# Linear attention and a gated MLP on one core: a new order for TensorE, K weights ahead of Q weights, and two tiles that are centred before the first projection

## The chip, the cores and the metric

The kernel runs on one core of a Trainium2 chip. The metric is device microseconds for one execution; the time before is the median of three runs. The engines of a core work side by side, each through its own list of instructions: TensorE (PE: matmuls and transposes), VectorE (DVE), ScalarE (ACT), GpSimd (POOL) and SyncE (SP), which here only issues DMA transfers. They wait for each other through semaphores. An order that differs between two kernels can therefore change the time although no instruction is added or taken away.

## The reference, cut to what matters

```python
def _layernorm(x):                     # over the last axis, eps = 1e-5
    return (x - mean(x)) / sqrt(var(x) + eps)

# x: 2048 x 448 bf16, 16 heads of 28; wqkv: 448 x 1344; wo: 448 x 448
q, k, v = split(_layernorm(x) @ wqkv)             # per head
phi = lambda t: where(t > 0, t + 1, exp(t)) + 1e-6
pq, pk = phi(q), phi(k)
kv  = pk^T v                                      # per head, 28 x 28, over all rows
z   = sum of pk over all rows
o   = (pq @ kv) / (pq . z + 1e-6)
h   = x + o @ wo
# w_gate, w_up: 448 x 1792; w_down: 1792 x 448
g, u = _layernorm(h) @ w_gate, _layernorm(h) @ w_up
out = h + (gelu(g) * u) @ w_down
```

`kv` needs all rows of K before any attention output can be formed. So the kernel first does K for all 16 tiles of 128 rows, and then attention output, gate/up and down projections tile by tile.

## The kernel before: the parts that matter

Every instruction is a task with a name, an engine and the buffers that it reads and writes. A table gives the order of the tasks on each engine; a task waits by semaphores for those on other engines that it depends on.

```python
ORDERS = ("26 34 32 43 41 63 ...", ...)     # PE, ACT, DVE, POOL, SP: task numbers

b_wqk = bufs("wqk", 2)                      # rows 0-383, and the tail of 64 rows
dma_x("sp", 0, 1)                           # x tile 0
tx1 = dma_x("act", 1, 2)                    # x tile 1
dma_w3("sp", wqk_sb, 0, 2 * D, b_wqk, "dwqk")     # Q and K weights, rows 0-383
dma_w1("sp", wqk_sb, 0, 2 * D, b_wqk, "dwqk_t")   # their tail
dma_x("sp", 2, 4); dma_x("sp", 4, 8); dma_x("sp", 8, 12); dma_x("sp", 12, 16)
# ... V weights, output weights

WARM = 40                                   # matmuls on a tile of ones
SEQ = "Q0 K0 K1 Q1 K2 Q2 K3 K4 K5 Q3 K6 K7 K8 ..."

def ln_tile(t):
    ln_stats(t, ...)                        # bn_stats, bn_aggr on DVE
    ln_rstd_act(t, ...)                     # ACT: Ln(var + eps), Exp(-0.5 * .)
    if t < N_PE_TR:                         # tiles 0 to 3
        # DVE: xnn = (x - mean) * rstd
        # PE: transpose by identity into two PSUM banks
        # ACT evacuates chunks 0 and 1, DVE chunks 2 and 3, into xnT
    else:
        # POOL: xnn = (x + negmean) * rstd
        # SP: transposing DMA xnn -> xnT

def k_tile(t):
    # PE: psK = xnT . wk (4 matmuls of 448 columns)
    # ACT: e1 = Exp(psK)
    # DVE: e1 = max(min(e1, 1 + EPS), 0)
    # DVE: pk = max(psK, EPS) + e1
    # PE: pt += xnn^T . pk (4 matmuls), accumulated over all tiles
def q_tile(t):
    # PE: psQ = xnT . wq;  ACT: eq = Exp(psQ), pq = Relu(psQ)
# ... (cut) kv and w2, the product of kv and wo

def a2_pair(p):                             # two tiles of attention output
    # DVE/POOL: pq, denominator, pqn; SP: transposing DMA oT (p > 0)
    # PE: out (8 matmuls, K = 112); DVE: h = x + out, statistics
    # POOL: normalisation; DVE: wrap (a copy); SP: transposing DMA hT

def gu_chunk(t0, nt):                       # groups of gate/up: 28 pairs of N=256 or 14 of N=512
    # PE: pairs on 64 rows each: psG on rows 0-63, psU on rows 64-127
    # ACT: gl = Gelu(psG); DVE: hh = psU * gl  (two halves)
def b2_tile(t):
    # PE: down, 14 matmuls of 448 columns; DVE: out = down + h; SP: store
```

Tiles 0 and 1, 2 and 3 form the gate/up groups 0 to 13 (28 pairs each), tiles 4 to 7 the groups 14 to 27, tiles 8 to 11 the groups 28 to 41, tiles 12 to 15 the groups 42 to 55 (14 pairs each). Gate and up have two PSUM banks each, used in turn. In the profile, L342 is the warm-up, L378 the transpose by TensorE, L404 a Q or K projection, L423 the accumulation of `pt`, L523 the attention output, L603 and L605 gate and up, L575 the down projection; L348 is the statistics, L370 the normalisation on VectorE, L390 the transposing DMA of a tile.

Of the kernel before, what the change touches and what calls it, by code (L numbers as in the profile page):

```python
# [5 lines left out]
BF16 = mybir.dt.bfloat16  # L6
F32 = mybir.dt.float32
ALU = mybir.AluOpType
# [7 lines left out]
    "26 34 32 43 41 63 66 71 76 50 52 61 59 79 84 70 87 116 75 99 83 111 91 126 103 138 150 115 130 162 174 142 187"  # L16
    " 200 154 213 219 229 166 245 178 191 235 204 217 179 233 249 192 205 218 234 250 254 251 291 257 295 297 293"
    " 299 263 315 266 317 319 260 320 269 278 275 272 333 337 356 434 439 387 444 449 454 459 418 464 506 472 516"
    " 511 526 521 469 490 531 536 578 583 588 562 544 593 598 603 608 613 675 541 618 623 628 633 638 643 706 651"
    " 648 657 654 722 727 732 737 742 747 752 757 762 767 772 777 782 787 804 809 814 795 792 801 798 819 824 829"  # L20
    " 834 839 844 849 854 859 864 869 874 877 880 883 886",
    "3 25 29 30 38 39 33 42 65 47 48 56 67 57 64 51 94 72 95 60 78 106 80 107 85 86 121 122 88 77 133 134 145 146"
    " 118 182 100 157 158 169 117 112 183 170 127 139 195 196 208 224 225 209 240 241 151 163 175 188 201 214 220"
    " 221 230 246 236 237 285 308 289 288 312 252 347 253 256 259 298 351 255 294 316 264 318 268 258 265 262 267"
    " 261 327 328 271 329 330 379 383 279 273 280 334 270 276 274 277 339 437 435 440 442 410 414 447 445 450 452"
    " 457 455 460 462 465 467 482 507 509 486 558 517 519 514 512 527 554 529 524 522 534 532 537 539 671 581 579"
    " 586 667 584 589 591 698 594 596 599 601 702 604 606 609 611 614 616 621 619 624 626 629 631 636 634 639 641"
    " 644 646 723 725 730 728 735 733 738 740 743 745 748 750 753 755 758 760 763 765 770 768 773 775 778 780 783"
    " 785 790 788 805 807 812 810 817 815 820 822 827 825 830 832 835 837 842 840 845 847 852 850 855 857 862 860"
    " 867 865 870 872",  # L30
    "27 28 36 37 31 40 35 44 45 54 46 55 104 49 92 58 93 68 53 69 105 73 62 74 119 131 120 143 81 144 180 132 181"
    " 89 82 167 155 90 156 168 101 193 102 222 194 113 223 114 340 128 206 129 238 207 303 239 140 141 301 152 302"
    " 153 164 165 176 177 189 202 342 190 343 215 216 341 203 231 372 232 247 248 304 374 373 375 287 286 305 307"
    " 309 290 311 310 313 346 292 350 296 378 348 352 314 300 349 353 321 405 322 324 323 325 475 326 331 382 332"
    " 335 384 336 380 385 381 338 403 406 404 360 357 361 358 409 362 359 413 436 438 411 415 441 443 412 416 367"
    " 476 448 446 388 547 549 451 453 391 370 389 458 390 477 392 548 478 456 461 393 463 419 693 550 485 481 422"
    " 466 468 508 510 420 553 423 487 424 401 691 398 557 421 662 483 518 520 488 515 559 513 663 484 429 560 555"
    " 523 525 692 432 670 660 528 530 661 473 491 494 556 694 535 533 538 540 666 495 582 580 492 470 587 672 493"
    " 496 697 585 590 566 563 668 669 673 564 592 567 565 595 597 701 568 699 600 703 602 605 607 704 545 612 504"
    " 700 615 573 617 679 676 610 680 677 542 678 681 622 620 625 627 576 501 630 632 637 635 640 707 710 642 645"  # L40
    " 708 711 709 712 686 647 652 649 717 720 658 724 726 655 731 729 736 734 739 741 744 746 689 749 751 754 756"
    " 759 761 764 766 771 769 774 776 779 781 784 786 791 789 806 808 813 811 818 816 796 793 799 802 821 823 828"
    " 826 831 833 836 838 843 841 846 848 853 851 856 858 863 861 868 866 871 873 875 878 881 884 887",
    "17 15 13 0 18 14 20 16 1 21 24 19 23 96 97 108 109 123 124 135 147 136 22 148 159 171 184 160 172 197 185 226"
    " 198 210 242 211 227 243 306 344 345 376 377 408 407 364 363 365 366 479 369 480 395 394 396 400 551 552 397"
    " 426 425 427 428 665 431 664 696 695 498 497 499 500 503 570 569 571 572 575 683 682 684 685 688 714 713 715"
    " 716 719",
    "2 4 5 6 7 8 9 10 11 12 98 110 125 137 149 161 173 186 199 212 228 244 281 282 283 284 354 386 355 417 368 371"
    " 402 399 489 430 433 474 561 471 674 505 574 705 543 546 502 577 687 653 718 721 650 656 659 690 797 794 800"
    " 803 879 876 882 885 888",  # L50
# [120 lines left out]
def bass_sequential_preLN__linear_attn_block__glu_gated_geglu__prompt_kernel(  # L171
# [11 lines left out]
    N_PE_TR = 4  # L183
    B1_CHUNKS = [2, 2, 4, 4, 4]
    WARM = 40
    T1_DVE = (0,)
    SEQ = "Q0 K0 K1 Q1 K2 Q2 K3 K4 K5 Q3 K6 K7 K8 K9 K10 K11 K12 K13 Q4 K14 Q5 K15 Q6 Q7 Q8 Q9 Q10 Q11 Q12 Q13 Q14 Q15"

    G = _Graph()
    es = ExitStack()  # L190
    with es:
        block = es.enter_context(nc.Block())

        def sb(name, shape, dt):
            return es.enter_context(nc.sbuf_tensor(name, shape, dt))

        x_sb = sb("x_sb", [128, T, D], BF16)
        xnn = sb("xnn", [128, XN_R, 512], BF16)
        xnT = sb("xnT", [128, T, 4, 128], BF16)
# [45 lines left out]
        def bufs(name, n):  # L245
            return [_Buf("%s%d" % (name, i)) for i in range(n)]

        b_x = bufs("x", T)
        b_xn = bufs("xn", XN_R)
        b_xnT = [bufs("xnT%d_" % t, 2) for t in range(T)]  # L250
        b_ones2 = _Buf("ones2")
        b_wqk, b_wv = bufs("wqk", 2), bufs("wv", 2)
# [48 lines left out]
        for dst, b, nm_ in ((wqk_sb, b_wqk, "wqkpad"), (wv_sb, b_wv, "wvpad")):  # L301
            op("pool", lambda e, dst=dst: e.memset(dst[:, 3, :], 0.0), [], [b[1]], nm_)  # L302
        dma_x("sp", 0, 1)
        tx1 = dma_x("act", 1, 2)
        dma_w3("sp", wqk_sb, 0, 2 * D, b_wqk, "dwqk")
        dma_w1("sp", wqk_sb, 0, 2 * D, b_wqk, "dwqk_t")
        dma_x("sp", 2, 4)
        dma_x("sp", 4, 8)
# [18 lines left out]
           [b_mtmp], [b_mask], "mask_b")  # L327
        op("pool", lambda e: e.memset(pt_sb[:, 3, :], 0.0), [], [b_pt[3]], "ptpad")
# [10 lines left out]
        def warm_fn(e):  # L339
            ins = None  # L340
            for _ in range(WARM):
                ins = e.matmul(ps[:, 3, 0:128], ones_bf[:], ones_bf[:], start=True, stop=True)  # L342
            return ins
        G.add("pe", warm_fn, r=[b_ones], w=[b_ps[3]], name="warm")
# [20 lines left out]
        def ln_tile(t):  # L365
# [3 lines left out]
            if t < N_PE_TR:  # L369
                op("dve", lambda e: e.tensor_scalar(xnn[:, i, 0:D], x_sb[:, t, :], mv1[:, t, 0:1], rs1[:, t:t + 1], ALU.subtract, ALU.mult),  # L370
                   [b_x[t], b_mv1[t], b_rs1[t]], [b_xn[i]], "normD_%d" % t)
                for h, (eng, k0, k1) in enumerate((("act", 0, 2), ("dve", 2, 4))):
                    bk = BK_TR[t % 2][h]

                    def ftr(e, k0=k0, k1=k1, bk=bk):
                        ins = None
                        for k in range(k0, k1):
                            ins = e.transpose(psb[:, bk, (k - k0) * 128:(k - k0 + 1) * 128], xnn[:, i, k * 128:(k + 1) * 128], ident[:])  # L378
                        return ins
                    G.add("pe", ftr, r=[b_xn[i], b_ones2, b_ident], w=[b_ps[bk]], name="tr%d_%d" % (h, t))  # L380
# [5 lines left out]
            else:  # L386
                ln_negm(t, t + 1, mv1, nm1, b_mv1, b_nm1, "1")
                op("pool", lambda e: e.tensor_scalar(xnn[:, i, 0:D], x_sb[:, t, :], nm1[:, t:t + 1], rs1[:, t:t + 1], ALU.add, ALU.mult),  # L388
                   [b_x[t], b_nm1[t], b_rs1[t]], [b_xn[i]], "normP_%d" % t)
                G.add("sp", lambda e: e.dma_start_transpose(xnT[:, t, :, :], xnn[:, i, :]), r=[b_xn[i], b_ones2], w=b_xnT[t], name="xT_%d" % t, kind="dma", after=[two])  # L390
# [16 lines left out]
        def proj_reads(t):  # L407
            return [(b_xnT[t][0], 0), (b_xnT[t][1], 2), (b_wqk[0], 0), (b_wqk[1], 3)]

        def k_tile(t):  # L410
# [3 lines left out]
            G.add("pe", lambda e, W: proj(e, W, t, bk, D), r=proj_reads(t), w=[b_ps[bk]], name="k_%d" % t, mw=True)  # L414
            eks.append(act_exp(lambda e: e.activation(e1[:, i, :], psK, AF.Exp), [b_ps[bk]], [b_e1[i]], "ek_%d" % t))  # L415
            op("dve", lambda e: e.tensor_scalar(e1[:, i, :], e1[:, i, :], 1.0 + EPS, 0.0, ALU.min, ALU.max), [b_e1[i]], [b_e1[i]], "ck_%d" % t)
            op("dve", lambda e: e.scalar_tensor_tensor(pk[:, ip, :], psK, EPS, e1[:, i, :], ALU.max, ALU.add), [b_ps[bk], b_e1[i]], [b_pk[ip]], "pk_%d" % t)  # L417
# [10 lines left out]
        def q_tile(t):  # L428
            bk = slot()
            G.add("pe", lambda e, W: proj(e, W, t, bk, 0), r=proj_reads(t), w=[b_ps[bk]], name="q_%d" % t, mw=True)  # L430
            act_exp(lambda e: e.activation(eq[:, t, :], ps[:, bk, 0:D], AF.Exp), [b_ps[bk]], [b_eq[t]], "eq_%d" % t)
            act_exp(lambda e: e.activation(pq[:, t, :], ps[:, bk, 0:D], AF.Relu), [b_ps[bk]], [b_pq[t]], "rq_%d" % t)
# [258 lines left out]
```

## Time and profile before

| | before |
|---|---|
| time, median of 3 | 194.2 us (193.75 to 194.72) |
| span of the profiled execution | 197.8 us |
| mean granted TensorE clock in it | 0.950 |
| TensorE matmuls | 193.7 us, 98% of the span |
| VectorE | 132.0 us, 67% |
| ScalarE | 78.1 us, 39% |
| GpSimd | 50.7 us, 26% |

Busy shares are averages over stages. The table by stage (us; share of it that VectorE is busy):

| window | what TensorE does | VectorE |
|---|---|---|
| 0 to 6.3 | warm-up, first transposes | 2.38 of 6.3 |
| 6.3 to 18.3 | first projections | 11.80 of 12.0 |
| 18.3 to 37.2 | the other K projections, pt | 16.87 of 18.9 |
| 37.2 to 51.4 | kv, last Q, first outputs | 13.82 of 14.2 |
| 51.4 to 64.5 | first gate/up groups, outputs | 12.75 of 13.1 |
| 64.5 to 106.5 | gate/up, outputs, downs | 37.12 of 42.0 |
| 106.5 to 197.7 | gate/up, downs | 37.26 of 91.2 |

A matmul is pipelined: its recorded duration (362 ns for 448 columns) is longer than the distance to the next one's start. So whether TensorE loses time is read from the starts. A line of the timeline has the start in us, the length in us, the engine, the line of the kernel, the operation and its tiles (written <- read); the bracket at the end, where there is one, is the idle time ahead of it and who ended it. The chain of waits is the chain of work that ended last, with start and length.

### The profile page before, as it was taken

Reading aid. Unit: us, or ns where it says so; the run is one execution under the profiler, and the core shown is the slowest. Engines: PE = TensorE matmul, PEld = TensorE weight load, DVE = VectorE, ACT = ScalarE, POOL = GpSimd, SP = SyncE. Lnnn points to the kernel's source line nnn. Section 1 sums busy time; section 2 is a strip of 40 time slices with the busy share of each in tenths; the row PEclk is TensorE's granted clock in tenths of the full one; section 3 lists DMA queues with packets and bytes.
Section 4 is the critical chain, followed back from the end, with each engine's and each line's share of the span. In section 5 each row is a group of like instructions: output and inputs, shape, how many; then the busy total and the mean of one; then the engine's idle time right before and its main releaser. Section 6 shows DMA issues by size and latency. Waiting matters only on the chain.

```text
span 197.8 us, 4145 instructions
## 1 busy us (share of the span) xinstructions
PE 193.7 (98%) x1572; PEld 106.9 (54%) x1572; DVE 132.0 (67%) x355; ACT 78.1 (39%) x226; POOL 50.7 (26%) x92
## 2 busy tenths in 40 slices
PE   7999999999999999999999999999999999999995
PEld 7554555555767776654454445444444454444454
DVE  3899988999999989988786537244445422444412
ACT  3797645599943324141330420023444200334200
POOL 7067710640451955235222024000000000000000
PEclk9999999999999999999999999999999999999999
DMA  6966449994587046420217272600200010100011
GB/s 194 375 174 88 94 96 209 221 215 63 102 291 124 16 50 117 102 53 23 56 26 153 57 56 52 133 21 30 46 0 3 0 46 4 46 0 3 0 46 46
DMA packets 35331, 16.97 MB, mean 86 GB/s; under 512 B 27696, under 2 KB 34032, under 8 KB 35312
## 3 DMA queue, kind: packets, MB, share of 16 engines
q1 hardware_dynamic: 35168, 16.60, 38.4%
q8 instruction: 12, 0.20, 0.4%
q10 hardware_dynamic: 144, 0.11, 0.2%
q14 instruction: 7, 0.06, 0.1%
HBM read 8.26 MB, written 1.84 MB: 51 GB/s over the span
## 4 chain that ended last, share of the span: by engine, by line
PE 90%; DMA 4%; DVE 4%; POOL 1%; issue 0%; DVEq 0%; POOLq 0%
PE ps L603 42%; PE ps L575 22%; PE ps L404 9%; PE ps L523 7%; PE ps L423 5%; PE ps L605 3%; DMA x_sb<-in_A_x_dram 2%; DVE st L348 2%; DMA xnT<-xnn 2%; DVE pk L417 1%; PE ps L471 0%; PE ps L462 0%; POOL wqk_sb L302 0%; PE ps L550 0%; DVE xnn L370 0%; DVE mv L349 0%
## 5 line engine op out<-in xcount | busy, mean ns | idle before, releaser
L605 PE MATMUL ps<-hnT,wgu_sb 64*128 64x512 bf16 (+1 forms) x490 | 89.9, 342 | 0.0
L603 PE MATMUL ps<-hnT,wgu_sb 64*128 64x512 bf16 (+1 forms) x490 | 89.6, 342 | 0.0
L623 ACT ACTIVATE gl<-ps 128x256 bf16<-128x256 f32 x112 | 37.1, 381 | 88.5 <-PE ps L605 86.4
L603 PEld LDWEIGHTS ps<-hnT,wgu_sb 64*128 64x128 bf16 x490 | 46.3, 96 | 35.1 <-issue 3.1
L625 DVE TENSOR_TENSOR hh<-ps,gl 128x256 bf16<-128x256 f32 x112 | 42.5, 416 | 34.0 <-ACT gl L623 33.7
L605 PEld LDWEIGHTS ps<-hnT,wgu_sb 64*128 64x128 bf16 x490 | 45.2, 96 | 3.7 <-DVE hh L625 0.5
L575 PE MATMUL ps<-wd_sb,hh 128*128 128x448 bf16 (+1 forms) x238 | 45.2, 351 | 0.0
L575 PEld LDWEIGHTS ps<-wd_sb,hh 128*128 128x128 bf16 x238 | 23.3, 99 | 21.1 <-issue 1.3
L404 PE MATMUL ps<-wqk_sb,xnT 128*128 128x448 bf16 x128 | 28.2, 362 | 0.1
L488 POOL TENSOR_TENSOR t<-pq,zbc 128x448 f32<-128x448 bf16 x15 | 16.6, 1115 | 33.3 <-DVE pq L484 20.5
L579 DVE TENSOR_TENSOR x_sb<-ps,x_sb 128x448 bf16<-128x448 f32 (+1 forms) x17 | 10.0, 592 | 19.6 <-PE ps L575 19.6
L348 DVE BATCH_NORM_STATS2 st<-x_sb 128x6 f32<-128x448 bf16 x32 | 19.1, 612 | 3.5 <-DMA x_sb<-in_A_x_dram 3.4
L404 PEld LDWEIGHTS ps<-wqk_sb,xnT 128*128 128x128 bf16 x128 | 12.3, 99 | 12.1 <-DMA xnT<-xnn 0.5
L423 PE MATMUL ps<-pk,xnn 128*128 128x448 bf16 x64 | 14.4, 363 | 0.0
L523 PE MATMUL ps<-w,pqnT 112*128 112x448 bf16 x64 | 14.1, 362 | 0.0
L558 POOL TENSOR_SCALAR hn<-x_sb,nm,rs 128x448 bf16<-128x448 bf16 x14 | 10.9, 779 | 8.1 <-DMA hnT<-hn 7.4
L529 DVE TENSOR_TENSOR x_sb<-ps,x_sb 128x448 bf16<-128x448 f32 x16 | 9.5, 617 | 3.8 <-PE ps L523 3.8
L415 ACT ACTIVATE e<-ps 128x448 bf16<-128x448 f32 x16 | 8.7, 541 | 5.4 <-PE ps L404 3.6
L417 DVE SCALAR_TENSOR_TENSOR pk<-ps,e 128x448 bf16<-128x448 f32 x16 | 9.9, 616 | 0.2
L388 POOL TENSOR_SCALAR xnn<-x_sb,nm,rs 128x448 bf16<-128x448 bf16 x12 | 9.0, 749 | 3.5 <-ACT rs L357 3.5
L423 PEld LDWEIGHTS ps<-pk,xnn 128*128 128x128 bf16 x64 | 6.5, 101 | 6.2
L495 DVE TENSOR_TENSOR pqn<-pq,rd 128x448 bf16<-128x448 bf16 x16 | 9.6, 622 | 0.0
(65 smaller groups left out, 125.0 us busy)
## 6 DMA issues: line engine op xcount, KB each, us to landing
out_dram<-x_sb SPq DMA_DIRECT2D x15, 112.0 KB, 1.7
wd_sb<-in_B_w_down_dram SPq DMA_DIRECT2D x1, 1568.0 KB, 7.7
x_sb<-in_A_x_dram SPq DMA_DIRECT2D x3, 448.0 KB, 5.4
wgu_sb<-in_B_w_gate_dram SPq DMA_DIRECT2D x1, 896.0 KB, 11.9
wgu_sb<-in_B_w_up_dram SPq DMA_DIRECT2D x1, 896.0 KB, 16.5
wqk_sb<-in_A_wqkv_dram SPq DMA_DIRECT2D x1, 672.0 KB, 4.8
wgu_sb<-in_B_w_gate_dram SPq DMA_DIRECT2D x1, 672.0 KB, 6.0
wgu_sb<-in_B_w_up_dram SPq DMA_DIRECT2D x1, 672.0 KB, 8.4
```

The source lines that it names most:

```text
L348: op("dve", lambda e: e.bn_stats(st[:, t, :], src_ap), [b_src], [b_st[t]], "bnst%s_%d" % (tag, t))
L404: ins = e.matmul(ps[:, bk, 0:D], xnT[:, t, k, :], wqk_sb[:, k, c0:c0 + D], start=(k == 0), stop=(k == 3))
L417: op("dve", lambda e: e.scalar_tensor_tensor(pk[:, ip, :], psK, EPS, e1[:, i, :], ALU.max, ALU.add), [b_ps[bk], b_e1[i]], [b_pk[ip]], "pk_ ...
L423: ins = e.matmul(ps[:, BK_PT[c], 0:D], xnn[:, t % XN_R, c * 128:(c + 1) * 128], pk[:, ip, :], start=(t == 0), stop=(t == T - 1))
L488: op(eng, lambda e, t=t, n=n: e.tensor_tensor(t1[:, n, :], pq[:, t, :], zbc[:, :], ALU.mult), [b_pq[t]] + b_z, [b_t1[n]], "t1%s_%d" % (eng ...
L523: ins = e.matmul(ps[:, BK_OUT[n], 0:D], pqnT[0:GW, i2, n, g, :], w2[:, g, :], start=(g == 0), stop=(g == NG - 1))
L558: op("pool", lambda e, t=t, sh=sh: e.tensor_scalar(hn[:, sh, 0:D], x_sb[:, t, :], nm2[:, t:t + 1], rs2[:, t:t + 1], ALU.add, ALU.mult), [b ...
L575: ins = e.matmul(psO, hh[:, j, (t % HR) * 128:(t % HR + 1) * 128], wd_sb[:, j, c0:c1], start=(j == 0), stop=(j == NJ - 1))
L603: e.matmul(psG[:, jj * N:(jj + 1) * N], wgu_sb[A_, k, j * 128:(j + 1) * 128], hnT[A_, ka_, c0:c0 + N], start=(k == 0), stop=(k == NK - 1))
L605: ins = e.matmul(psU[:, jj * N:(jj + 1) * N], wgu_sb[B_, k, j * 128:(j + 1) * 128], hnT[B_, kb_, c0:c0 + N], start=(k == 0), stop=(k == NK ...
L623: G.add("act", lambda e, gi=gi, cs_=cs_, psG=psG: e.activation(gl[:, gi, cs_], psG[:, cs_], AF.Gelu_apprx_tanh), r=[b_ps[BK_G[i]]], w=[b_g ...
L625: op("dve", lambda e, dst=dst, srcU=srcU, srcL=srcL: e.tensor_tensor(dst, srcU, srcL, ALU.mult), [b_ps[BK_U[i]], b_glh], [b_ar[j_][t % HR] ...
```

## The change

Four things.

1. **The orders of all engines are new.** On TensorE before, the outputs of tiles 4-5, 6-7, 8-9, 10-11, 12-13 and 14-15 stand behind gate/up groups 1, 5, 11, 16, 21 and 27, and downs behind 7, 11, 16, 21, 27, 44 and 55. After, outputs stand behind groups 3, 6, 13, 23, 27 and 27 and downs behind 6, 13, 27 and 55: 4-5 behind 3; 6-7 with downs 1 and 0 behind 6; 8-9 with downs 2 and 3 behind 13; 10-11 behind 23; 12-13, down 4, 14-15, downs 5 to 7 behind 27; downs 8 to 15 at the end. It is for fewer changes between the 64-row pairs and the full array.
2. **K weights come first.** The Q/K weights are loaded in two halves, K ahead of Q, with the load of x tile 2 between them and the other x loads split finer. The first projection is K's.
3. **Tiles 0 and 1 are only centred** ahead of their transpose and projections. The factor rstd is applied by ScalarE as the scale of Exp and Relu (both read rows of the tile along partitions). This takes rstd off the way to the first projection. `pt` still needs the normalised tile, which GpSimd now forms.
4. **The warm-up** is 34 matmuls and two more tasks of 3.

```diff
-    "26 34 32 43 41 63 ..."            # all five orders are new
+    "30 31 32 38 40 49 ..."
@@
+    CEN = (0, 1)
-    WARM = 40
+    WARM, WARM2, NW2 = 34, 3, 2
-    SEQ = "Q0 K0 K1 Q1 K2 Q2 K3 ..."
+    SEQ = "K0 K1 Q0 K2 Q1 Q2 K3 ..."
@@
-        b_wqk, b_wv = bufs("wqk", 2), bufs("wv", 2)
+        b_wqt = _Buf("wqt")
+        b_wqk, b_wv = [[_Buf("wq"), b_wqt], [_Buf("wk"), b_wqt]], bufs("wv", 2)
@@
-        dma_w3("sp", wqk_sb, 0, 2 * D, b_wqk, "dwqk")
-        dma_w1("sp", wqk_sb, 0, 2 * D, b_wqk, "dwqk_t")
-        dma_x("sp", 2, 4)
-        dma_x("sp", 4, 8)
+        dma_wqk(1)
+        dma_w1("sp", wqk_sb, 0, 2 * D, [None, b_wqt], "dwqk_t")
+        dma_x("sp", 2, 3)
+        dma_wqk(0)
+        dma_x("sp", 3, 4)
+        dma_x("sp", 4, 6)
+        dma_x("sp", 6, 8)
@@
+        warm(WARM, "warm")
+        for i in range(NW2):
+            warm(WARM2, "warm2_%d" % i)
@@ ln_tile
+                if t in CEN:
+                    op("dve", lambda e: e.tensor_scalar(xc[:, t % 2, 0:D], x_sb[:, t, :], mv1[:, t, 0:1], None, ALU.subtract), ...)
@@
-            else:
+            if t >= N_PE_TR or t in CEN:
                 ln_negm(...)
                 op("pool", ... normP)
@@ k_tile
+            sc = rs1[:, t:t + 1] if t in CEN else 1.0
+            ... activation(e1, psK, AF.Exp, scale=sc)
+            if t in CEN:
+                act_exp(... activation(pk, psK, AF.Relu, scale=sc))
+                op("dve", ... e1 = min(e1, 1.0) + EPS)
+                op("dve", ... pk = pk + e1)
@@ q_tile
+            ... Exp and Relu with scale=sc
```

`...` stands for what is cut. Apart from this the kernel is the same.

## The prediction

> **What bounds the kernel now.** I read the page's busy shares and its chain of work first, then the timeline of TensorE, then the chain and the timeline of the first 19 us.
>
> ```profile
> PE 193.7 (98%) x1572; PEld 106.9 (54%) x1572; DVE 132.0 (67%) x355; ACT 78.1 (39%) x226; POOL 50.7 (26%) x92
> ...
> PE 90%; DMA 4%; DVE 4%; POOL 1%; issue 0%; DVEq 0%; POOLq 0%
> ```
>
> TensorE is busy for 98% of the span and carries 90% of the chain. No busy time is removed by this change: the 1572 matmuls stay. So the gain can only be sought where TensorE's starts are further apart than its own pace. That pace, in starts: 4 matmuls of 448 columns take 0.79 us, and one gate-up group (14 pairs of 512 columns, or 28 of 256) takes 1.57 us. I went through the stream task by task and kept what is above that.
>
> First loss: the change of array shape. Gate/up matmuls run in pairs on 64 rows; all others use 128 rows (112 for the attention output).
>
> ```profile
> 101.77 0.39 PE L605 MATMUL ps<-hnT,wgu_sb 64*128 64x512 bf16 x1
> 102.09 1.74 PE L523 MATMUL ps<-w,pqnT 112*128 112x448 bf16 x8
> ...
> 92.46 1.55 PE L575 MATMUL ps<-wd_sb,hh 128*128 128x448 bf16 x7
> 93.94 0.39 PE L603 MATMUL ps<-hnT,wgu_sb 64*128 64x512 bf16 x1
> ```
>
> A 64-row pair is followed 0.32 us later by the first full one, where pairs follow each other at 0.22: 0.10 lost on leaving. On entering, the seventh down matmul starts at 92.46 + 6 x 0.197 = 93.64 and the first pair at 93.94: 0.30 instead of 0.197, again 0.10. One visit outside the gate-up groups costs about 0.19 us.
>
> Second loss: inside gate-up. Group 5 takes 1.74 us, group 16 1.76 and group 21 1.86. Less the 1.57 and 0.10 for leaving, 0.07 + 0.09 + 0.18 = 0.35 us of waits for VectorE's products.
>
> Third loss: the head.
>
> ```profile
> 1.11 4.30 PE L342 MATMUL ps<-ones_bf 128*128 128x128 bf16 x40 [1.11 <-POOL ones_bf L315]
> ...
> 4.24 0.29 ACT L355 ACTIVATE ln<-mv,eps_t 128x1 f32<-128x1 f32 x1 [1.75 <-DVE mv L349]
> ...
> 5.30 0.20 ACT L357 ACTIVATE rs<-ln 128x1 f32<-128x1 f32 x1
> ...
> 5.61 0.40 DVE L370 TENSOR_SCALAR xnn<-x_sb,mv,rs 128x448 bf16<-128x448 bf16 x1 [0.39 <-ACT rs L357]
> ...
> 6.07 0.40 PE L378 MATMUL ps<-ident,xnn 128*128 128x128 bf16 x4 [0.32 <-DVE xnn L370]
> ...
> 6.31 3.30 PE L404 MATMUL ps<-wqk_sb,xnT 128*128 128x448 bf16 x16
> ```
>
> The first projection starts at 6.31 because TensorE's order puts the transposes of tile 1 ahead of it, and they wait for tile 1's normalisation, which waits for two ACT steps. The weights only just come in time: from the issues, the Q/K block lands at 6.03 and its tail at 6.29.
>
> ```profile
> 2.48 4.26 DMA x_sb<-in_A_x_dram
> ...
> 6.77 1.15 DVE st L348 x2
> ...
> 14.40 3.85 DMA xnT<-xnn
> 18.25 0.05 issue
> 18.30 0.96 PE ps L404 x4
> ```
>
> The chain of that stretch runs beside TensorE: tiles 2 and 3 land at 6.74, VectorE is full until 14.4, then tile 6's transposing DMA takes 3.85 us and the K projection of tile 6 waits 0.22 us for it. From 6.31 to 18.30 TensorE loses 0.27 (tile 3's transpose) and these 0.22.
>
> **What the Trainium skill says.** "TensorEngine Tiling (Array Packing)", Key Properties: a change of tiling mode drains TensorE. The trace agrees, at 0.10 us each way. "TensorE: Matmul & The Clock Gate", What's actually happening: TensorE starts at 1.2 GHz and gets 2.4 GHz after about 3.4 us of work; here the 40 warm-up matmuls start 0.107 us apart, the transposes after 5.37 about 0.055. "VectorE: DVE Perf Modes", The perf-mode tier table: a two-tensor operation runs at 2x from bf16 in SBUF and at 1x with a PSUM operand; here 0.61 us with PSUM (the K feature) and 0.38 us without (the Q addition). "ScalarE: Activation LUTs", What ACT_TABLE_LOAD costs: a per-partition pointer operand adds about 93 ns; here Ln, with a pointer bias, takes 0.29 us, the small Exp without one 0.20.
>
> **The change part by part.** I translated both order tables into task names.
>
> 1. Orders behind the head. Gate-up groups before run as 0-1, 2-5, 6-7, 8-11, 12-16, 17-21, 22-27, 28-44, 45-55: nine runs. After: 0-3, 4-6, 7-13, 14-23, 24-27, 28-55: six. Three visits fewer: 3 x 0.19 = 0.57 us saved. Outputs 4-5 leave the place behind group 1, 10-11 move from behind group 16 to behind 23, 12-13 from behind 21 to stand beside 14-15 and the downs 4 to 7; the downs 8 to 11 leave the place behind group 44 for the end. The arithmetic is the same.
>    Does VectorE keep up without the output in between? Groups 0-3 take 6.3 us. The new order gives it eight products at about 0.34 from start to start (2.7), two additions for h and two statistics (4 x 0.54), two reductions (1.1), two Q additions (0.6) and small ones: near 7 us, of which the last part falls under the 1.6 us output that follows group 3. Walking it, group 0's bank is free some 0.2 us before group 2 needs it: tight, but no stall. I count half of the 0.35 us of waits as gone: 0.2.
>    hT of tiles 8-11 is needed at group 28, about 20 us after output 10-11: hidden.
>
> 2. Tiles 0 and 1 only centred. Off the path: the two ACT steps. New on it: both statistics come first on VectorE. From 3.37: statistics to 4.50, aggregates to 4.73, centred tile 0 at 4.65-5.02 and tile 1 at 4.95-5.30 (a scalar operation at 0.37-0.40, as the normalisation). Tile 0 gains 0.2 us, tile 1 0.7. Off the path: two normalisations on POOL (0.71 each, idle there until 10.08), two Relu of K on ACT (0.54 each plus about 0.09 for the pointer scale), two additions at 0.38 on VectorE for two at 0.61.
>
> 3. Warm-up. 34 + 2 x 3 = 40 matmuls as before, in front of the first transposes, with no wait. The ones tile is now first on POOL, so they start about 0.1 earlier and end near 5.26. No gain of their own, and they cap tile 0's.
>
> 4. K weights first. After x0 and x1 (3.34 and 3.53) the old 672 KB took until 6.03. Half of it lands near 4.75, the tail near 5.1, tile 2 near 5.45 instead of 6.74; the Q half near 6.7, tile 3 near 7.1, tiles 4-5 near 7.65, 6-7 near 8.2. Estimates from the old block's rate (some 270 KB/us) and 0.28 us per x tile.
>
> The head walked: transposes 5.27-5.75; ACT's copy of tile 0 at 5.65-6.03; K0 at 6.06, where Q0 was 6.31 (VectorE's half of tile 0 ends 6.28, in time for the third matmul). K1, Q0 to 8.42. Tile 2's normalisation waits on VectorE for the statistics of tiles 3 and 5, so its transposes come at 8.72: 0.3 us lost. From there I find no wait up to K6: at 17.84, with tile 6's transposing DMA issued near 14.85 and landed at 17.4 if it takes the usual 2.6 us. Before, K6 stood at 18.30. Gain 0.45.
>
> Sum: 0.57 + 0.2 + 0.45 = 1.2 us. 194.2 - 1.2 = 193.0 us.
>
> **The rivals.**
> - The transposing DMA takes K6's start. If it again needs 3.85 us, it lands at 18.7 and the head gains nothing or loses 0.4. For it: VectorE's and ACT's work ahead of tile 6's normalisation is no shorter than before. Against: the other transposes took 2.4 to 2.6. It would make 193.5 to 193.9.
> - VectorE becomes the bound in the longer runs of gate-up: it is busy 12.75 of 13.1 us from 51.4 to 64.5. Each product late costs its delay; 1 to 2 us in all would give 194 to 195. Against it: the outputs that made its extra work come later, and it is under half busy from 106.
> - The head gains everything: no wait at tile 2 or 3, 0.8 to 1 us, and no wait at all in gate-up. That would be 192.3.
>
> **Range and chances.** The switches are almost sure (0.5 to 0.6), the head lies between -0.4 and +1.0, gate-up between -1 and +0.35. That gives 191.8 to 194.4. A move of 2% is 3.9 us, over three times everything I can find: faster 0.03, same 0.955, slower 0.015.
>
> **What would show it.** TensorE's timeline should show five outside visits between the first and last gate-up run, each with 0.10 us on both sides; the first K projection near 6.06, the first Q near 7.6, tile 2's transposes near 8.7, K6 near 17.8; the chain of waits should still be TensorE from there. I am wrong if K6 starts at 18.3 or later, if gate-up groups other than those ahead of a visit take more than 1.6 us, or if the clock steps up later than the transposes.

## The result and the profile after

| | before | after |
|---|---|---|
| time, median of 6 runs each | 194.23 us (193.75 to 194.72) | 195.65 us (195.01 to 196.43) |
| ratio after / before, 95% interval | | 1.0075 [1.0046, 1.0103] |

The change costs 1.4 us (0.9 to 2.0 by the interval). 193.0 was predicted, with 191.8 to 194.4 as the range: a move of some tenths of a percent was the right order of size, but its direction was wrong.

The profile of before shown ahead of the prediction was taken at a mean granted clock of 0.950, which stretches TensorE's work and so covers waits behind it (the wait at the K projection of tile 6 is 0.22 us there and 0.72 at full clock). All comparisons below use a second profile of the kernel before, with the clock at 1.000. First its page, busy time and shares of the chain of waits:

```profile
PE 187.6 (97%) x1572; PEld 106.8 (55%) x1572; DVE 131.2 (68%) x355; ACT 77.8 (40%) x226; POOL 50.9 (26%) x92
...
PE 84%; DVE 9%; DMA 3%; ACT 2%; issue 1%; DVEq 0%; ACTq 0%
```

The same two lines of the page of after:

```profile
PE 187.8 (97%) x1572; PEld 101.7 (52%) x1572; DVE 131.5 (68%) x355; ACT 78.7 (41%) x228; POOL 52.1 (27%) x97
...
PE 86%; ACT 5%; DVE 4%; DMA 2%; issue 1%; POOL 1%; SPq 0%; DVEq 0%; ACTq 0%; POOLq 0%
```

TensorE's busy time is the same, as it must be: only the gaps between its starts can differ. So I divided the span at five starts on TensorE, and in each stretch compared its starts with the full-clock pace (4 matmuls of 448 columns 0.757 us, a gate/up group 1.51 to 1.53). "After" is the profile of the result; "after, 2nd" is another execution of the same kernel, 1.2 us shorter.

| stretch (us) | before | after | after, 2nd |
|---|---|---|---|
| start of the first projection | 6.40 (Q0) | 6.03 (K0) | 6.27 (K0) |
| from there to the K projection of tile 6 | 12.07 | 12.90 | 12.42 |
| K6 to the first `kv` matmul | 19.68 | 20.74 | 19.89 |
| `kv` to `w2` | 1.70 | 2.40 | 2.39 |
| `w2` to the first gate/up group | 10.85 | 10.59 | 10.59 |
| first gate/up group to the end | 141.74 | 141.32 | 141.34 |
| span | 192.45 | 193.97 | 192.90 |

Below the first row each entry is a difference of two starts. The tail, which has most of the new order, gains 0.4. Everything else that changes sign is ahead of the first gate/up group: the head, a stretch behind K6 that is slow in one execution and not in the other, and the two microseconds around `kv`.

**The head.** The timeline of after, 5.2 to 7.9 us (start, length, engine, line, operation, tiles, count; in brackets the idle time ahead and its end). L399 is now the transpose by TensorE, L426 a Q or K projection, L406 VectorE's evacuation of a transpose, L364 the statistics:

```profile
5.20 0.61 PE L399 MATMUL ps<-ident,xc 128*128 128x128 bf16 x8
6.03 0.54 PE L426 MATMUL ps<-wqk_sb,xnT 128*128 128x448 bf16 x2 [0.23 <-ACT rs L373]
6.44 0.63 DVE L364 BATCH_NORM_STATS2 st<-x_sb 128x6 f32<-128x448 bf16 x1 [1.15 <-DMA x_sb<-in_A_x_dram]
6.99 0.47 DVE L406 COPY xnT<-ps 128x256 bf16<-128x256 bf16 x2
7.32 2.06 PE L426 MATMUL ps<-wqk_sb,xnT 128*128 128x448 bf16 x10 [0.75 <-DVE xnT L406]
```

K0 starts at 6.03 (6.06 predicted), does two matmuls, and then stands until 7.32. Its third matmul needs VectorE's half of tile 0, whose transpose has been there since 5.8. But VectorE's list has the statistics of tile 2 ahead of that copy, and they wait 1.15 us for the load of tile 2. In the second profile of after that load landed earlier, at 5.61, and K0 ran through.

What comes next on the way to K6 is in the chain of waits of the second profile of after (start, length, work):

```profile
11.91 4.38 DMA xnT<-xnn
16.29 0.14 issue
16.43 0.92 PE ps L426 x4
```

and, the same view of before at full clock:

```profile
14.38 4.05 DMA xnT<-xnn
18.43 0.05 issue
18.47 0.93 PE ps L404 x4
```

Before, the one slow transposing DMA is that of tile 6, and K6 waits for it. After, the slow one is that of tile 4, two tiles earlier, and K4 waits for it. In the profile of after, a second one is late, that of tile 13. The timeline of TensorE around it:

```profile
27.25 0.92 PE L426 MATMUL ps<-wqk_sb,xnT 128*128 128x448 bf16 x4
28.89 0.92 PE L426 MATMUL ps<-wqk_sb,xnT 128*128 128x448 bf16 x4 [0.72 <-ACT e L439]
```

From K12 to K13 it is 1.64 us instead of 0.757. The bracket names the Exp that ended just then, that of tile 12, for which K13 does not wait (by the program it waits for that of tile 9, long done). The transposing DMA of tile 13, for which it does wait, took 3.5 us from its issue and landed at 28.76, just ahead of that start.

**Around `kv`.** The timeline of the second profile of after (L519 is GpSimd's product for a denominator, L493 `kv`, L526 the product `pqn = pq * rd`, which I call pn, L497 the masked copy of `kv`, kvm, L502 the product `w2`):

```profile
38.58 1.00 PE L493 MATMUL ps<-pt_sb,wv_sb 128*112 128x112 bf16 x16
38.87 1.03 POOL L519 TENSOR_TENSOR t<-pq,zbc 128x448 f32<-128x448 bf16 x1
38.96 1.42 DVE L526 TENSOR_TENSOR pqn<-pq,rd 128x448 bf16<-128x448 bf16 x1
40.31 0.61 DVE L497 TENSOR_TENSOR kvm<-ps,mask 112x448 bf16<-112x448 f32 x1
40.97 0.96 PE L502 MATMUL ps<-wo_sb,kvm 112*112 112x448 bf16 x4 [0.63 <-DVE kvm L497]
```

The same of before (GpSimd's product is L488, `pn` L495, `kvm` L466):

```profile
38.01 0.62 DVE L495 TENSOR_TENSOR pqn<-pq,rd 128x448 bf16<-128x448 bf16 x1
38.16 0.99 PE L462 MATMUL ps<-pt_sb,wv_sb 128*112 128x112 bf16 x16
38.17 1.35 POOL L488 TENSOR_TENSOR t<-pq,zbc 128x448 f32<-128x448 bf16 x1 [0.46 <-DVE den L491]
39.18 0.62 DVE L466 TENSOR_TENSOR kvm<-ps,mask 112x448 bf16<-112x448 f32 x1
39.86 0.96 PE L471 MATMUL ps<-wo_sb,kvm 112*112 112x448 bf16 x4
```

The same product takes 1.42 us after and 0.62 before, and `kvm`, next in VectorE's list, is late by the difference. In after it starts at 38.96 while one of GpSimd's products is running, 38.87 to 39.90; before it starts between two of them, of which the second begins at 38.17.

**The tail.** TensorE's timeline of after at the output of tiles 10-11 (L634 and L636 gate and up, L554 the output):

```profile
105.43 0.38 PE L636 MATMUL ps<-hnT,wgu_sb 64*128 64x512 bf16 x1
105.74 1.69 PE L554 MATMUL ps<-w,pqnT 112*128 112x448 bf16 x8
107.36 0.39 PE L634 MATMUL ps<-hnT,wgu_sb 64*128 64x512 bf16 x1
```

0.31 from the last pair to the first output where pairs follow at 0.21, and 8 outputs at 0.189 from 105.74 end at 107.25, 0.11 ahead of the next pair: 0.10 to 0.11 on each side, as before. There are five such visits, as predicted.

### The profile page after: what moved, and what is told of

Its sections match the earlier page's. It is cut to its first block, busy times and chain, and to the rows that moved or that the text cites. A ratio compares the mean times of both kernels' runs of the same rounds, so it can differ in the third digit from the quotient of the medians.

```text
span 194.0 us, 4159 instructions
## 1 busy us (share of the span) xinstructions
PE 187.8 (97%) x1572; PEld 101.7 (52%) x1572; DVE 131.5 (68%) x355; ACT 78.7 (41%) x228; POOL 52.1 (27%) x97
## 4 chain that ended last, share of the span: by engine, by line
PE 86%; ACT 5%; DVE 4%; DMA 2%; issue 1%; POOL 1%; SPq 0%; DVEq 0%; ACTq 0%; POOLq 0%
PE ps L636 29%; PE ps L606 22%; PE ps L634 16%; PE ps L426 9%; PE ps L554 7%; PE ps L452 3%; DMA x_sb<-in_A_x_dram 2%; ACT e L439 2%; ACT eq L462 1%; ACT pq L463 1%; DVE pqn L526 1%; DVE den L522 1%; ACT ln L371 1%; PE ps L502 0%; POOL wqk_sb L306 0%
## 5 line engine op out<-in xcount | busy, mean ns | idle before, releaser
L636 PE MATMUL ps<-hnT,wgu_sb 64*128 64x512 bf16 (+1 forms) x490 | 87.0, 334 | 0.0
L634 PE MATMUL ps<-hnT,wgu_sb 64*128 64x512 bf16 (+1 forms) x490 | 86.4, 334 | 0.0
L636 PEld LDWEIGHTS ps<-hnT,wgu_sb 64*128 64x128 bf16 x490 | 42.7, 94 | 29.1 <-DVE hh L656 9.5
L634 PEld LDWEIGHTS ps<-hnT,wgu_sb 64*128 64x128 bf16 x490 | 43.3, 94 | 10.7 <-issue 1.9
L606 PE MATMUL ps<-wd_sb,hh 128*128 128x448 bf16 (+1 forms) x238 | 43.2, 342 | 0.0
L426 PE MATMUL ps<-wqk_sb,xnT 128*128 128x448 bf16 x128 | 27.9, 353 | 1.8 <-DVE xnT L406 0.8
L519 POOL TENSOR_TENSOR t<-pq,zbc 128x448 f32<-128x448 bf16 x15 | 16.5, 1112 | 30.3 <-DVE pq L515 16.8
L364 DVE BATCH_NORM_STATS2 st<-x_sb 128x6 f32<-128x448 bf16 x32 | 19.1, 616 | 5.1 <-DMA x_sb<-in_A_x_dram 4.8
L426 PEld LDWEIGHTS ps<-wqk_sb,xnT 128*128 128x128 bf16 x128 | 11.7, 98 | 14.0 <-DVE pk L446 1.4
L554 PE MATMUL ps<-w,pqnT 112*128 112x448 bf16 x64 | 13.6, 353 | 0.0
L409 POOL TENSOR_SCALAR xnn<-x_sb,nm,rs 128x448 bf16<-128x448 bf16 x14 | 10.4, 745 | 4.9 <-ACT rs L373 4.1
L526 DVE TENSOR_TENSOR pqn<-pq,rd 128x448 bf16<-128x448 bf16 x16 | 10.4, 662 | 0.0
L376 POOL TENSOR_SCALAR ln<-mv 128x2 f32<-128x2 f32 x7 | 1.9, 275 | 31.5 <-DVE mv L365 31.3
L589 POOL TENSOR_SCALAR hn<-x_sb,nm,rs 128x448 bf16<-128x448 bf16 x14 | 10.0, 718 | 0.5
L439 ACT ACTIVATE e<-ps 128x448 bf16<-128x448 f32 x14 | 7.6, 540 | 5.8 <-PE ps L426 4.6
L522 DVE TENSOR_REDUCE den<-t 128x16 f32<-128x448 f32 x16 | 9.6, 603 | 0.0
```

The costliest lines, as they stand in the source:

```text
L364: op("dve", lambda e: e.bn_stats(st[:, t, :], src_ap), [b_src], [b_st[t]], "bnst%s_%d" % (tag, t))
L426: ins = e.matmul(ps[:, bk, 0:D], xnT[:, t, k, :], wqk_sb[:, k, c0:c0 + D], start=(k == 0), stop=(k == 3))
L519: op(eng, lambda e, t=t, n=n: e.tensor_tensor(t1[:, n, :], pq[:, t, :], zbc[:, :], ALU.mult), [b_pq[t]] + b_z, [b_t1[n]], "t1%s_%d" % (eng ...
L522: op("dve", lambda e, n=n, i=i: e.tensor_reduce(den[:, i, :], t1[:, n, :].rearrange("p (h d) -> p h d", h=H), AX.X, ALU.add), [b_t1[n]], [ ...
L526: op("dve", lambda e, t=t, n=n, i=i, i2=i2: e.tensor_tensor(pqn[:, i2, n, :, 0:GW].rearrange("p g (h d) -> p g h d", h=4), pq[:, t, :].rea ...
L554: ins = e.matmul(ps[:, BK_OUT[n], 0:D], pqnT[0:GW, i2, n, g, :], w2[:, g, :], start=(g == 0), stop=(g == NG - 1))
```

## The experiments

Each kernel is compared with the kernel before in the same series; intervals are 95%. Task names: `k_4` is the K projection of tile 4, `pt4_4` its four matmuls into `pt`; `evxD_0` VectorE's evacuation for tile 0; `bnst1_2` the statistics of tile 2; `t1p_4` and `dr_2` GpSimd's product for tile 4 and VectorE's reduction for tile 2; `rd_1` the reciprocal of tile 1.

**Both kernels again (b_again, a_again).** No edit. The first profiles of the two had different clocks.

> The kernel before once more, for a profile at the full TensorE clock: its first profile had 0.950, the one of the changed kernel 1.0, so waits can't be compared between them. Expected: span near 192.3 us (194.2 less some 2 us ahead of the first instruction), 4 matmuls of 448 columns 0.757 us apart instead of 0.79. Theory A (the head was lost): the waits of TensorE from the first projection to the last task before the gate-up groups add to under 1.5 us, against 3.7 in the changed kernel. Theory B (the longer gate-up runs were lost): they add to about 3 us here too, and the waits inside gate-up are under 0.5 us.

> The changed kernel once more, for a second profile: which waits come again. If the load of x tile 2 again lands near 6.4 us and the third matmul of the first K projection waits 0.9 us for it, that wait belongs to the order (theory A). If the multiplication pn_0 on VectorE again takes 1.43 us instead of 0.61, and the transposing DMA of tile 13 again comes 0.9 us late, they belong to the kernel too; if not, they were chance and can't explain a difference that all six timed runs show. Time 195 to 196.4.

Measured: 194.17 and 194.81 us, both at clock 1.000. They are the columns "before" and "after, 2nd" of the table. From the first projection to K6 TensorE loses 1.0 us in the kernel before (0.29 ahead of tile 3's transposes, 0.72 at K6), where the first profile showed 0.27 and 0.22; to the first gate/up group it is 1.7. How much of this stretch is waiting for VectorE and the DMA was hidden by the slower clock.

**The halves (t_tail, h_head).** The five order tables split at the first gate/up group.

```diff
 t_tail: program, K/Q loads, warm-up and orders of before up to the last transposes ahead of gate/up;
-        orders of before from there on
+        orders of after from there on
 h_head: the reverse, all of after's head, orders of before behind it
```

> The program and the head of the kernel before, with the changed order only from the second pair's attention output on (first gate-up group to the end): six gate-up runs instead of nine. Theory A: 193.6 us, that is 0.5 to 0.6 under the kernel before. Theory B: 195 or more, all of the loss and more.

> The changed head (K weights first, two tiles centred, new orders up to the last transposes before the gate-up groups) with the old order behind it. Theory A: 196.0 to 196.3 us, all of the loss and the switches that the changed tail saves. Theory B: 194.2 or less.

Measured: t_tail 194.60 against 194.50, 1.0005 [0.9995, 1.0016]; h_head 196.98, 1.0128 [1.0094, 1.0163]. The loss lies ahead of the first gate/up group. Neither size is clean. In t_tail ScalarE's order from before leaves four Q evacuations between the first `hT` and the first Gelu (after has two), and groups 1 and 2 wait 0.30 and 0.42 for it. In h_head the output of tiles 4-5 stands at its early place behind group 1 while the work for it comes at the late place of the new order: a wait of 1.32 us that neither kernel has. So these two say where, not how much.

**kvm ahead of the product (a_kvm).** VectorE's order of after:

```diff
-rd_1 pn_0 kvm dr_3
+rd_1 kvm pn_0 dr_3
```

> The changed kernel with one move on VectorE: the masking of kv (kvm) ahead of pn_0. Both profiles of the changed kernel show pn_0 at 1.42 us instead of 0.62, because it starts while GpSimd is inside t1p_4, and TensorE waiting 0.8 us for kvm behind it. Theory C (the order at kv is a loss of its own): TensorE's wait ahead of the output-weight product falls from 0.79 to under 0.1 us and the time by 0.6 to 0.8, to a ratio of about 1.004. Theory D (TensorE only meets the next wait): ratio unchanged at 1.0075.

Measured: 195.10 against 194.44, 1.0035 [1.0021, 1.0049]. Its timeline at this place:

```profile
39.67 0.62 DVE L497 TENSOR_TENSOR kvm<-ps,mask 112x448 bf16<-112x448 f32 x1 [0.59 <-PE ps L493]
40.21 0.62 DVE L526 TENSOR_TENSOR pqn<-pq,rd 128x448 bf16<-128x448 bf16 x1
40.35 0.96 PE L502 MATMUL ps<-wo_sb,kvm 112*112 112x448 bf16 x4
```

`kvm` starts as soon as `kv` is out, pn takes 0.62 again, and `w2` starts 1.72 us behind `kv`. Between after's 1.0075 and this lie 0.40 points, 0.78 us, with wide intervals. The profiles account for 0.4 us: `w2` comes 0.67 earlier against `kv`, but the stretch from `w2` to gate/up is 10.85 again instead of 10.59, as smaller waits come back (0.27 in all around the two transposes ahead of the first outputs, 0.11 at the output of tiles 2-3).

**Why the product is long (a_dr2).** In VectorE's order of after pn_0 is put ahead of a reduction, so that it meets another of GpSimd's products.

```diff
-evpD_2 dr_2 rd_0 rd_1 pn_0 kvm
+evpD_2 rd_0 pn_0 dr_2 rd_1 kvm
```

> The changed kernel with pn_0 ahead of the reduction dr_2 on VectorE, nothing else. GpSimd's t1p_4 writes the buffer that dr_2 reads, so it can't start before dr_2 is through, and pn_0 no longer starts inside it. If VectorE and GpSimd exclude each other for these two operations: pn_0 takes 0.62 us instead of 1.42, and TensorE's wait for kvm falls from 0.79 to under 0.2 us. If pn_0 is slow for another reason (its operands, its place behind the reciprocals): it stays at 1.4 us.

Measured: 194.38 in one execution. VectorE's and GpSimd's lines:

```profile
36.77 2.04 POOL L519 TENSOR_TENSOR t<-pq,zbc 128x448 f32<-128x448 bf16 x2
38.33 0.95 DVE L526 TENSOR_TENSOR pqn<-pq,rd 128x448 bf16<-128x448 bf16 x1
```

The product was not at 0.62 as expected: it now started within the product ahead of the one meant, which ran to 38.80, and ended at 39.28, 0.48 behind it. In the second profile of after GpSimd's ended at 39.90 and pn_0 at 40.38, in the first at 40.99 and 41.47: 0.48 each time. Before, pn_0 was first, and it is GpSimd's product, begun at 38.17, that takes 1.35 instead of 1.04. Whoever comes second ends a fixed time behind the first (GpSimd's 0.90 behind pn_0, in both profiles of before). This is what the Trainium skill states in "SBUF — State Buffer", section "SBUF: two separate sides": VectorE, in an operation with two inputs in SBUF, and GpSimd share one port pair as an exclusive lock that is held for the whole instruction. The trace agrees: 1.42 and 0.95 us for a 0.62 us product, by how much of GpSimd's 1.04 was left. `kvm` reads one operand from PSUM and isn't stretched: in a_kvm it took 0.62 beside a GpSimd product that ran until 39.95.

**Evacuation ahead of the statistics (a_evx).**

```diff
-cen_1 bnst1_2 evxD_0 evxD_1
+cen_1 evxD_0 evxD_1 bnst1_2
```

> The changed kernel with one move on VectorE: its two evacuations of tiles 0 and 1 ahead of the statistics of tile 2, which wait for the load of tile 2 (landed at 5.6, 6.4 and 6.9 us in three profiles). Theory C: the first K projection runs through from about 6.0 us whatever the load does, instead of stopping up to 1.1 us at its third matmul; the time falls by 0.3 to 0.9 us, ratio 1.003 to 1.006. Theory D: TensorE then waits for tile 2's transposes instead, ratio 1.0075.

Measured: 195.77, 1.0063 [1.0045, 1.0080]; against after's 1.0075 [1.0046, 1.0103] a difference of 0.1%, which is within the intervals. K0's wait falls from 0.92 to 0.30, but in the profile nothing is gained by it: K4 starts at 16.72, as it did (16.66), when tile 4's transposing DMA lands.

```profile
16.72 0.92 PE L426 MATMUL ps<-wqk_sb,xnT 128*128 128x448 bf16 x4 [0.45 <-DMA xnT<-xnn]
```

The wait at K0 was visible, and slack.

**No centred tiles (a_nocen), one block of weights (a_wqk1).**

```diff
 a_nocen
-CEN = (0, 1)
+CEN = ()        # tiles 0 and 1 normalised as before, the orders fitted to it
 a_wqk1
-dma_wqk(1) ... dma_x("sp", 2, 3); dma_wqk(0); dma_x("sp", 3, 4); ...
+one Q/K block of 672 KB, then x 2-3, x 4-7, as before
```

> The changed kernel without the centring: tiles 0 and 1 normalised in full on VectorE as before, no Relu of K on ScalarE, no normalisation of them on GpSimd (their order on VectorE and ScalarE adapted, since K's bank is again freed by VectorE). If the centring does what it is for: the transposes of tile 1 come 0.5 us later and the time rises by 0.2 to 0.5 us. If its extra ScalarE work (two Relu at 0.63 us, pointer scales) costs more than it brings: the time falls, ratio under 1.0065.

> The changed kernel with the old transfers: Q and K weights in one block of 672 KB ahead of x tiles 2-3 and 4-7 in one transfer each. Theory E (the finer pieces spread the 16 parts of a transfer: the slowest part comes 0.7 to 1.4 us behind the middle one, and V and output weights land at 14.2 to 15.9 us instead of 12.9): ratio falls to about 1.003, and the output weights land near 13. Against it: the load of tile 2 lands at 6.7, so with VectorE's order kept the first projection can't pass its third matmul before 7.6 and the time is the same or 0.3 us longer, ratio 1.0075 to 1.009.

Measured: a_nocen 195.91, 1.0076 [1.0050, 1.0102]; a_wqk1 196.13, 1.0083 [1.0062, 1.0105]. Against after's 1.0075 no gain by the centring shows, and 0.15 us by K first; but with these intervals a gain or loss of up to some 0.7 us in either would not show, and the two were not taken out together in the new order. The warm-up was not tried alone. In a_wqk1 the output weights were in at 12.66 (15.90 in after, 12.88 before), yet tile 4's transposing DMA, issued at 12.68, still took 4.04 us: it is slow without late bulk loads too.

**Both repairs (a_both), and the old head (b_mid).** a_both has the edits of a_kvm and a_evx. b_mid has the program and the orders of before up to the last matmuls into `pt`, then those of after with `kvm` ahead of pn_0: no K first, no centring.

```diff
 b_mid
-orders of before behind the last pt
+orders of after behind the last pt, with rd_1 kvm pn_0 on VectorE
```

> The changed kernel with both moves on VectorE: kvm ahead of pn_0, and the evacuations of tiles 0 and 1 ahead of tile 2's statistics. If the two losses add: ratio near 1.002 (1.0075 less 0.004 less 0.0012). If the second only moves TensorE's wait on to tile 2 and to the transposing DMA of tile 4: 1.0035, as with the first alone.

> The program of the kernel before and its order up to the last accumulation of pt; behind it the changed order (from the Q projections beside kv to the end) with kvm ahead of pn_0. No K-first load, no centring. If the loss sits in the head and in pn_0, and the changed tail is good for 0.4 us when the order ahead of it fits: 193.6 to 193.9 us, ratio 0.996 to 0.9975. If the tail brings nothing even so: 1.000.

Measured in one series: a_both 195.03 (19 runs; a twentieth, at a lower clock, took 198.59 and is left out), 1.0025 [1.0011, 1.0039]; b_mid 194.26 against 194.57, 0.9982 [0.9970, 0.9993]. b_mid beats both kernels, by less than the 193.6 to 193.9 expected. The timeline of a_both shows the start of the head as predicted:

```profile
5.54 0.51 DVE L406 COPY xnT<-ps 128x256 bf16<-128x256 bf16 x2 [0.32 <-PE ps L399]
5.95 2.43 PE L426 MATMUL ps<-wqk_sb,xnT 128*128 128x448 bf16 x12 [0.23 <-ACT rs L373]
5.97 0.62 DVE L364 BATCH_NORM_STATS2 st<-x_sb 128x6 f32<-128x448 bf16 x1
```

K0, K1 and Q0 run through from 5.95, the copies ahead of the statistics. K4 starts at 16.27 all the same, 0.16 earlier than in the second profile of after, where K0 started 0.3 later. The pages of b_mid and, for its middle, its timeline:

```profile
PE 188.0 (98%) x1572; PEld 102.5 (53%) x1572; DVE 131.1 (68%) x355; ACT 77.8 (40%) x226; POOL 50.2 (26%) x92
...
PE 91%; DMA 3%; ACT 2%; DVE 1%; POOL 0%; issue 0%; DVEq 0%
```

```profile
39.43 0.62 DVE L466 TENSOR_TENSOR kvm<-ps,mask 112x448 bf16<-112x448 f32 x1 [0.58 <-PE ps L462]
40.11 0.96 PE L471 MATMUL ps<-wo_sb,kvm 112*112 112x448 bf16 x4
```

From after to b_mid the ratio goes in steps: 1.0075, with `kvm` first 1.0035, with the copies first too 1.0025, with the old head 0.9982. The new head is worth 0.43 points, or 0.84 us, in the wrong direction; this step lies within one series and is clear of the intervals. That of `kvm`, 0.40, is about as large, and that of the copies, 0.10, is within noise.

**The same kernel in other executions (a_look2, a_look3).** No edit. If the new head's loss is K4's and K13's wait, the time less these must not change.

> The changed kernel, third profile. If the late transposing DMA of tile 13 makes the slow runs: a time above 195.3 us goes with a wait of 0.7 us or more ahead of the K projection of tile 13, a time under 195 without it. The wait of 0.79 us for kvm is there in either case.

> The changed kernel, fourth profile; expectation as for the third.

Measured: 194.78 and 195.24. Neither is over 195.3, so the slow side of the expectation wasn't met with here; the profile of after, at 195.99, has it.

| profile | time | K4 starts | waits from K4 to `kv` | time less both |
|---|---|---|---|---|
| after, 2nd | 194.81 | 16.43 | none | 178.38 |
| a_look2 | 194.78 | 16.38 | none | 178.40 |
| a_look3 | 195.24 | 16.88 | none | 178.36 |
| after | 195.99 | 16.66 | 0.89 (tile 13) | 178.44 |

From run to run the changed kernel differs in two things, when K4 starts and whether tile 13 waits; what is left agrees within 0.1 us. In the first three K4 starts 0.13 to 0.14 us behind the landing of tile 4's transposing DMA: 16.29, 16.25, 16.74; in the fourth too (16.52). For a_both the same difference is 194.32 - 16.27 = 178.05, and for b_mid, with 16.31 as the place of K4 (K6's start less three times 0.757), 194.39 - 16.31 = 178.08. So these two are equal from there on, and their fastest runs are near each other (194.23 and 194.10); it is the typical run of the new head that is later.

**Moving the wait (b_pt4, b_q4, a_pt9).** Three attempts to put work of TensorE's under the late DMA.

```diff
 b_pt4, from b_mid
-pt4_3 k_6 pt4_4
+pt4_3 pt4_4 k_6
 b_q4, from b_mid
-K5 Q3 K6 ... K13 Q4 K14
+K5 Q3 Q4 K6 ... K13 K14
 a_pt9, from a_both
-k_12 k_13 pt4_9
+k_12 pt4_9 k_13
```

> The old head with the changed middle and tail and kvm ahead of pn_0 (ratio 0.9982 before this move), with the accumulation pt4_4 ahead of the K projection of tile 6 on TensorE. That projection waits 0.67 us for its transposing DMA; pt4_4 has its operand about 0.35 us after the wait begins, so 0.3 us of the wait is filled. If that holds: ratio 0.9965. If the next K projections are late by what was gained: 0.998.

> As the last one, and the Q projection of tile 4 moved ahead of the K projection of tile 6, with its evacuations on ScalarE. The K projection of tile 6 waits 0.7 us for its transposing DMA in the kernel before (profile at full clock), and 0.76 us of work fits there. If that wait is a fixed arrival: 0.5 to 0.7 us less than the last one, ratio 0.993 to 0.994. If TensorE's lead is eaten by the next transposing DMA or by the bank order: same as the last one.

> As the kernel with both moves on VectorE, and on TensorE the accumulation pt4_9 ahead of the K projection of tile 13, which then needs its transposing DMA 0.76 us later. In three profiles of changed-head kernels with times near 196 us that DMA landed 3.5 us after its issue instead of 2.5, and TensorE waited 0.7 to 1.05 us; in four with times of 194.3 to 194.8 it did not. If this wait makes the difference between those times: the median falls from 195.1 to 194.5 or less, ratio 0.9995 or less, and the spread shrinks. If the times differ for another reason: 1.0025.

Measured: b_pt4 194.26 against 194.43, 0.9987 [0.9978, 0.9996]; b_q4 194.78 against 194.57, 1.0015 [1.0001, 1.0028]; a_pt9 195.56 against 194.43, 1.0055 [1.0033, 1.0077]. All three missed. In b_pt4 the wait at K6 goes, but pt4_4 in its place waits 0.45 for VectorE, and K9 0.27. In b_q4 the profiled execution, the slowest of its series, has tile 4's DMA at 4.2 us, a wait of 1.30 at K4, 0.60 at K14 and 0.54 at K15. In a_pt9 K4 waits 1.0 and new waits stand at K15 (0.13) and the Q projection behind it (0.56); its profile has no late tile 13, so it doesn't say what that wait is worth on average. In these three profiles a TensorE task moved ahead of the wait only moves it: the tiles come through VectorE, SyncE and the DMA no sooner.

## Why the prediction was wrong

**"K0 at 6.06 ... VectorE's half of tile 0 ends 6.28, in time for the third matmul."** K0 was right (6.03), the second half failed. I counted tile 2's load as landed at 5.45, from a rate. In the trace its 16 parts land between 4.97 and 6.42 in after, and the statistics need the last one; over the profiles of the changed head that was 5.5 to 6.9. VectorE's statistics of tile 2 stand ahead of the copy in its order; with the load at 5.45 they would have been out of the way. The loss at K0 is 0.92 us in after, none in its second profile; undoing it brought 0.1%, within noise, because of the next point.

**"From there I find no wait up to K6: at 17.84, with tile 6's transposing DMA ... if it takes the usual 2.6 us."** This step carried the 0.45 us gain and failed most. Tile 6's transposing DMA did take the assumed time (15.08 to 17.57 in the second profile of after), but there is a wait ahead of K6 that the walk did not have, at K4: the slow transposing DMA did not go away, it moved to tile 4 (4.0 to 4.7 us from issue in every profile of the changed head), and K4 waits for it, 0.70 us in the second profile. K6 started at 18.65 to 19.14 in the four profiles of the changed kernel, against 18.47 before and 17.84 predicted; 18.3 or later was named ahead as a sign of being wrong. The first rival had the mechanism, a slow DMA that takes the gain, but set it on tile 6 and stopped at a loss of 0.4; with tile 13's wait, which came in some executions, the typical loss is 0.84. None of the gains ahead of it (centring, K first, an unbroken K0) shows in the time: each is measured as 0.2 us or less, within noise.

**The middle was not looked at.** Part 1 checked gate/up and the outputs, not the two microseconds around `kv`, where the new order only puts other Q projections in the same places on TensorE. There pn_0 moved into GpSimd's product, and `kvm` behind it came late: 0.69 us on TensorE's path, of which 0.26 come back behind it, where a wait of 0.38 at the Q projection between the first two transposes of the outputs is gone.

**The tail's "0.57 + 0.2".** The measured gain is 0.40. The three visits fewer are right: each side of a visit still costs 0.10, five visits are left of eight. "Half of the 0.35 us of waits as gone" failed. At full clock, the gate/up groups before lose 2.76 us in all, of which 8 visits at 0.2 are 1.6 and leaving at the end 0.1: 1.05 of waits. After it is 2.34 less 1.0 and 0.1: 1.2. The waits grew by 0.2 instead of falling by 0.2. In the list of waits before, weight loads for gate/up held up by VectorE's products (total us, times, longest):

```profile
PEld ps L605 <- DVE hh L625: 2.2, 11, 0.4
```

and after:

```profile
PEld ps L636 <- DVE hh L656: 9.5, 31, 0.5
```

Almost three times as many groups meet a bank that VectorE hasn't freed; most of it is covered by matmuls still queued, but groups 23, 33 and 55 lose 0.31, 0.18 and 0.31 (0.10 of the first and the last is for leaving). Groups 2 and 33, neither ahead of a visit, take 1.66 and 1.69, the second of the signs that were named. That is the second rival's mechanism at a tenth of its size.

**The reading that misled.** "The K projection of tile 6 waits 0.22 us for it" was read at a clock of 0.950. At full clock it is 0.72, and TensorE loses 1.0 from the first projection to K6, not 0.49. Had I known, the stretch up to K6 would have been seen as one bound by transfers and VectorE, where an earlier first projection buys no time.

The sum as it should have been, in us: visits -0.57, gate/up waits +0.17, `kvm` less what comes back +0.4, head with tile 13 +0.84, statistics ahead of the copies +0.1 to +0.2 (the difference of a_kvm and a_both, and of after and a_evx, both within noise): +0.9 to +1.0. By the runs it is 194.23 x (1.0075 - 1) = 1.46, with 0.9 to 2.0 as its interval. That the new head and `kvm` lose and the tail gains is settled by the runs; the 0.5 between the two sums is within what six runs leave open, and may lie in how often the two DMAs are late, which the profile of one execution can't give.

**What stays open.** Why the slow transposing DMA is that of tile 4 with the new head, and why tile 13's is late in some executions. In every profile a 16 KB transfer of instructions starts while the slow one is in flight: at 15.3 to 16.0 us with the old head, when tile 6's is, and at 13.7 to 15.0 with the new, when tile 4's is; tile 13's, where it is late, with one of 8 KB that starts 1.8 to 2.3 us after its issue; where it is on time, that one starts 2.2 us after its issue or later. In two profiles with the old head it came at 13.1 and 13.4, and there tile 4's took 4.2 and 4.4. Over all 18 profiles, each of the 79 transposing DMAs of `xnT` (of 216) that took over 2.6 us overlaps such a transfer; of the 137 that took less, only 3 have one that starts in their flight more than 0.3 us ahead of the landing. That is a coincidence in time, if a close one: no run moved that transfer alone, so it isn't shown as the cause.

## What to carry to other kernels

A gain at the start of a stretch is worth nothing if the stretch ends on something else: follow the stretch to its last wait (here a transposing DMA) before counting it, and read waits only from a profile at full clock. When an order changes, look at what an instruction meets on the other engines at its new place, above all two-input VectorE products beside GpSimd ones, and keep what TensorE waits for ahead of work that can be stretched. Count a load as there when its last part is.

## What was not expected of the hardware

A VectorE product that meets a running GpSimd one shows as one long instruction (1.42 and 0.95 us for 0.62), not as idle time ahead of it: such a wait is seen only by comparing the lengths of single instructions of one group. The transposing DMA of one and the same size takes 2.5 us from issue to landing, or 4.0 to 4.7, in the same execution. And of a wait of 0.92 us on TensorE, plainly visible in the timeline, two thirds could be taken away for 0.1% of time, within noise.
